# A max of three products rewritten around a product made once: x(W1Wo) + max(0, x(W2-W1), x(W3-W1))Wo

## The chip, the core and the metric

One core of one Trainium2 chip runs the whole program. Its engines have queues of their own: TensorE (PE, with PEld for its weight loads), VectorE (DVE), ScalarE (ACT), GpSimd (POOL) and SyncE (SP), which here only issues DMAs. The metric is the device time of one execution in microseconds, the median of several runs. All numbers are float32.

## The reference

A delta-rule attention block feeds a feed-forward block with a max over three products. Batch 4, 8 heads, 768 positions, head size 48; then 3072 tokens of 384 features, hidden size 768.

```python
for t in range(S):
    y[:, :, t] = einsum('bhd,bhde->bhe', q[:, :, t], state)
    v_old = einsum('bhde,bhd->bhe', state, kt)          # kt: normalized key
    state = state + bt * einsum('bhd,bhe->bhde', kt, vt - v_old)
x = y.transpose(0, 2, 1, 3).reshape(3072, 384)
h = maximum(maximum(x @ w1, x @ w2), x @ w3)
out = h @ w_out
```

## The kernel before

**Groups.** The sequence is cut into chunks of 64 positions. A "unit" of the recurrence is one chunk of all batches and heads, two units make a group, and a group is 512 tokens. There are six groups, 0 to 5. `ffn(m)` computes the feed-forward part of group m; it is a generator which yields after every step, and between its steps the attention of the next group is issued. So matmuls of the two parts alternate in TensorE's one queue in an order written out by hand.

**The feed-forward part.** `hidden(f, lo, w)` makes one of six tiles h (128 hidden features by 512 tokens): for each of w1, w2, w3 three matmuls into a PSUM tile p_h (L884), then a ScalarE copy for the first (L892) and a VectorE max for the other two (L894). After the six tiles, four output tiles p_o of 128 tokens are made by six matmuls each (L908), copied by ScalarE to o_sb (L916) and written to memory (L919). p_h and p_o share a PSUM ring of two tiles. A group from 1 on has 18 hidden steps and 4 output steps, numbered i = 0 to 21. Group 0 runs 18 half-wide hidden steps, 9 whole ones and 4 output steps, i = 0 to 30; weights are still being unpacked there.

**The attention around it.** The table `LINKS` says which pieces of attention are issued after step i of a group. A letter is a function, the digit a unit (or one of four key blocks). Those that matter here:

- k, q: `old_k`, `old_q`, the products of keys and queries with the state (p_k, p_q, L737); k also subtracts on VectorE (v_t, L749). s: `step`, the state update (p_s, st). u, z, j: `new`, `join_z`, `join_u`, the products that make u. y: `to_y` makes y (p_y, L805, and VectorE, L807). x: `y_blocks` sends y to memory as y_x (L837).
- w: `read_y` loads y back in another layout as y_q (L846). X: `turn_y` transposes y_q into half of xt, the next group's input, on VectorE (L857). Beside group 0 x is `to_x` instead, with TensorE transposes (p_x, L819), and w and X are not used.
- K, V: loads of later keys and values (L115, L131). p: `prep_sums` squares a unit's keys on ScalarE (ksq, L282), sums them on VectorE (L283) and exchanges the sums by DMA (ksum, L288). P: `prep_values` makes norms of them (L260 to L265) and scales v_t on GpSimd (L292).
- L, N: `load_blocks` loads blocks of keys on SyncE and of queries on GpSimd into tiles called turned (L401), from a ring of five tiles that y_q uses too. t: `turn_blocks` transposes them on VectorE (kqt, L417). g: `gram` multiplies them (p_g, L443) and sends the result to memory (at_d, L473).

**The triangular solve.** `solve(m)` reads at_d as x_bl and does, on VectorE alone, a set-up (L534 to L550) and 31 steps of two operations each (L564, L568), then sends y_d (L590) and loads ut from it (L599). `some(solving, n)` issues n of its steps. The loop over groups starts it after step 10 of groups 1 to 3 and spreads its steps over the rest of the group; its last two pieces, the ut loads, fall at the end. Group 4 issues no solve and no key loads, and group 5 has no attention beside it.

Of the kernel before, what the change touches and what calls it, by code (L numbers as in the profile page):

```python
# [12 lines left out]
ALU = mybir.AluOpType  # L13
# [8 lines left out]
def kernel(  # L22
# [31 lines left out]
    nc = tc.nc  # L54
# [3 lines left out]
    DM = H * D  # L58
    DFF = moe_w1.shape[1]
    KT = DM // 128  # L60
    FT = DFF // 128
# [16 lines left out]
    def ps_ffn(shape, name):  # L78
        return psum.tile(shape, FP32, name=name, tag="ffn", bufs=2)

    def ps_two(name):
        return psum.tile([128, 2, 512], FP32, name=name, tag="two", bufs=3)
# [4 lines left out]
    ident = const.tile([128, 128], FP32, name="ident")  # L87
# [16 lines left out]
    def rows(bb):  # L104
        return slice(C * bb, C * (bb + 1))
# [67 lines left out]
    for bb in range(2):  # L173
        nc.gpsimd.affine_select(
            out=mask[rows(bb)], in_=mask[rows(bb)], pattern=[[1, C]], base=-1,
# [10 lines left out]
    w_sb = [const.tile([128, KT, DFF], FP32, name=f"w{i}_sb") for i in range(3)]  # L186
    wo_sb = const.tile([128, FT, DM], FP32, name="wo_sb")
# [15 lines left out]
    def fetch(queue=nc.scalar):  # L203
        if fetched[0] < len(pieces):
            _, src, (a, b) = pieces[fetched[0]]
            st = work.tile([128, 2 * 384], U32, name="w_bits", bufs=5)
            queue.dma_start(
                out=st.rearrange("p (a b) -> p a b", a=a), in_=src
            )
            staged.append(st)  # L210
            fetched[0] += 1
# [63 lines left out]
    def prep_sums(c):  # L275


        ksum, kflip = small("ksum", 2, H), small("kflip", H)
        for g in range(2):
            kk = kpad[(2 * c + g) % NK][:, :, 0:D]  # L280
            ksq = work.tile([128, H, D], FP32, name="ksq", tag="o_sb")
            nc.scalar.square(ksq, kk)  # L282
            nc.vector.tensor_reduce(  # L283
                out=kflip if g else ksum[:, 0], in_=ksq,
                axis=mybir.AxisListType.X, op=ALU.add,
            )
        for bb in range(2):
            nc.sync.dma_start(out=ksum[rows(bb), 1], in_=kflip[rows(1 - bb)])  # L288
        sums[c] = ksum
# [59 lines left out]
    def square(name):  # L349
        return work.tile([128, H, C], FP32, name=name, tag="square", bufs=17)  # L350
# [39 lines left out]
    def load_blocks(n):  # L390
        c, g = divmod(n, 2)
        for i in range(2):
            t = turned[n, i] = work.tile(
                [128, 2, TURNED], FP32, name="turned", tag="w_bits", bufs=5
            )
            nc.gpsimd.memset(t[:, :, TURNED - 48 : TURNED], 0.0)  # L396
            for bb in range(2):
                for par in range(2):
                    for db in range(2):
                        p0, at = DP * par + 32 * db, 32 * (1 - db)  # L400
                        (nc.sync, nc.gpsimd)[i].dma_start(  # L401
                            out=t[p0 : p0 + 32, bb, at : at + NP * 2 * D].rearrange(
                                "p (j x) -> p j x", j=NP
                            ),
                            in_=(k, q)[i][
                                2 * bb + g, :, c * C : (c + 1) * C, :
                            ].rearrange(
                                "(j two) (r tb) d -> two r j (tb d)", two=2, tb=2
                            )[par],
                        )  # L410
# [459 lines left out]
            nc.vector.tensor_copy(to[:, 1], of[:, 1])  # L870


    def ffn(m):
        xt = xts[m]
        hs = {}

        def hidden(f, lo, w):
            if f not in hs:
                hs[f] = square("h").rearrange("p h c -> p (h c)")
            h = hs[f][:, lo : lo + w]  # L880
            for i in range(3):
                p_h = ps_ffn([128, TOK], "p_h")[:, 0:w]
                for t in range(KT):
                    nc.tensor.matmul(  # L884
                        p_h,
                        w_sb[i][:, t, f * 128 : (f + 1) * 128],
                        xt[:, t, lo : lo + w],
                        start=(t == 0),
                        stop=(t == KT - 1),
                    )  # L890
                if i == 0:
                    nc.scalar.copy(h, p_h)  # L892
                else:
                    nc.vector.tensor_tensor(out=h, in0=h, in1=p_h, op=ALU.max)  # L894
                yield


        early = FT // 2 if m == 0 else 0
        for lo in (0, TOK // 2):
            for f in range(early):  # L900
                yield from hidden(f, lo, TOK // 2)
        for f in range(early, FT):
            yield from hidden(f, 0, TOK)
        for i in range(4):
            cc, g = divmod(i, 2)
            p_o = ps_ffn([128, DM], "p_o")
            for f in range(FT):
                nc.tensor.matmul(  # L908
                    p_o,
                    hs[f][:, i * 128 : (i + 1) * 128],  # L910
                    wo_sb[:, f],
                    start=(f == 0),
                    stop=(f == FT - 1),
                )
            o_sb = work.tile([128, DM], FP32, name="o_sb")
            nc.scalar.copy(o_sb, p_o)  # L916
            for bb in range(2):
                tok0 = (2 * bb + g) * S + (2 * m + cc) * C
                nc.sync.dma_start(out=out[tok0 : tok0 + C, :], in_=o_sb[rows(bb)])  # L919
            yield  # L920
# [3 lines left out]
    def some(gen, n):  # L924
        for _ in range(n):
            if next(gen, gen) is gen:
                break
# [72 lines left out]
    for c in range(2):  # L1000
# [29 lines left out]

    LINKS = {
        0: "k0 q0 t0 L2", 1: "g0 t1 L3", 2: "g1 d0", 3: "z0 d1", 4: "z1 t2",
        5: "j0 g2", 6: "j1 t3", 7: "u0 g3", 9: "s0", 10: "y0", 11: "k1 q1 x0",
        12: "w0 V0", 13: "u1", 14: "K0 K1 V1", 15: "y1 x1 X0", 16: "K2 K3 p0",
        17: "s1 w1 p1", 18: "N0 P0", 19: "X1 P1", 20: "N1",
    }
    EARLY_LINKS = {
        9: "k0 q0", 10: "e0", 11: "e1 t0", 12: "f0 t1", 13: "f1 d0 g0",
# [20 lines left out]
    def links(m, names):  # L1059
        for name in names.split():  # L1060
            f, i = name[0], int(name[1])
            if f in RECURS and m < GROUPS:
                RECURS[f](2 * m + i)
            elif f in MADE and m + 1 < GROUPS:
                MADE[f](2 * (m + 1) + i)
            elif f in UNIT and m + 1 < GROUPS:
                UNIT[f](4 * (m + 1) + i)
            elif f == "N" and m + 2 < GROUPS:
                load_blocks(4 * (m + 2) + i)

    def queries(names):
        for name in names.split():
            f, n = name[0], int(name[1])
            if f not in OF_KEYS:
                links(0, name)
                continue
            OF_KEYS[f](n)
            if f == "T" and n + 3 < 11:
                load_q(n + 3)
# [4 lines left out]
    for i, _ in enumerate(ffn(0)):  # L1084
        if i - 1 in CONVERTED:
            fetch(nc.sync)
        queries(FIRST.get(i, ""))
        links(1, EARLY_LINKS.get(i, ""))
        if i in CONVERTED:
            some(conv, 1)  # L1090
        if i in (1, 2):
            prep_sums(i + 1)
        if i in (4, 5, 6):
            some(solving, (4, 2, 1)[i - 4])
        if i in (5, 7):
            prep_values(i // 2)
        if 7 <= i < 11:
            load_k(i + 1)
        if i == 0:
            load_v(3)  # L1100
        if i == 12:
            load_q(11)
        if i in (10, 18):
            load_v(4 + i // 18)
        if i in (11, 15):
            prep_sums(4 + i // 15)
        if i in (14, 20):
            prep_values(4 + i // 20)
        if i == 18:
            blocks(2)  # L1110
        if i == 21:
            solving = solve(2)
            some(solving, 1)
        if 21 < i < 27:
            some(solving, 3)
        if i >= 27:
            some(solving, 4 if i < 30 else 5)
        if i in (27, 28):
            load_blocks(i - 15)


    RECURS.update(x=y_blocks, w=read_y, X=turn_y)
    UNIT.update(t=turn_blocks)
    for m in range(1, GROUPS):
        for i, _ in enumerate(ffn(m)):
            if i < 2:
                some(solving, 1)
            if m + 2 < GROUPS:
                if i == 8:
                    blocks(m + 2)  # L1130
                if i == 10:
                    solving = solve(m + 2)
            steps = 4 if i >= 18 else 3
            if i > 10:
                some(solving, steps - 2)
            links(m + 1, LINKS.get(i, ""))
            if 10 <= i < 20:
                some(solving, 2)
    by_hand.close()
# [28 lines left out]
```

## Time and profile before

| | us |
|---|---|
| median of three runs | 574.99 |
| lowest, highest | 573.28, 579.36 |
| span of the profiled execution | 571.2 |
| PE busy | 536.1 |
| DVE busy | 358.1 |
| ACT busy | 145.4 |
| POOL busy | 127.1 |

The span runs from the first to the last instruction of the profiled execution; what lies around it is not in it. Where the groups stand, from the timeline of TensorE (start of the group's first p_h, in us from the span's start):

| group | 1 | 2 | 3 | 4 | 5 | end of the last p_o |
|---|---|---|---|---|---|---|
| start | 178.99 | 261.02 | 344.48 | 428.75 | 504.90 | 566.9 |

In the page, "busy" is the sum of an engine's instructions; a timeline line has start, duration, engine, line of the kernel, operation, output and inputs, shapes, count, and in square brackets how long the engine stood idle before it and what released it. SPq is SyncE's queue, where a duration is the time to issue.

### The profile page before, as it was taken

How to read it: one execution, taken by the hardware profiler on the slowest of the kernel's cores; microseconds unless marked ns; L12 is line 12 of the kernel's file. 1: busy time of each engine (PE TensorE's matmuls, PEld its weight loads, DVE VectorE, ACT ScalarE, POOL GpSimd, SP SyncE). 2: the span in 40 equal slices, each digit the busy share in tenths (PEclk: the TensorE clock that was granted, in tenths of full speed). 3: DMA queues.
4: the chain of work that ended last, by engine and by line, in shares of the span. 5: the costliest groups of instructions: out<-in, count | busy, mean ns of one | idle time of the engine just before them, and what ended most of it. 6: DMA issues, size and time to landing. Idle time of an engine off the chain costs nothing.

```text
span 571.2 us, 18729 instructions
## 1 busy us (share of the span) xinstructions
PE 536.1 (94%) x8102; PEld 317.1 (56%) x8102; DVE 358.1 (63%) x785; ACT 145.4 (25%) x282; POOL 127.1 (22%) x224
## 2 busy tenths in 40 slices
PE   6678779889999999999999999999999999999997
PEld 5567657765555555555555464555555555544453
DVE  6888998786997645996637995637994432201110
ACT  4455544455302221212121111221112201010001
POOL 7225235144540530016430017300011000000000
PEclk9656899989999999999999999999999999999999
DMA  8874467756035632645642846632834001310002
GB/s 111 173 162 122 94 161 137 176 120 159 9 74 129 134 71 74 115 113 143 136 84 67 136 99 161 125 57 64 136 88 90 3 12 48 78 33 1 0 0 55
DMA packets 149057, 53.54 MB, mean 94 GB/s; under 512 B 133296, under 2 KB 145392, under 8 KB 148976
## 3 DMA queue, kind: packets, MB, share of 16 engines
q1 hardware_dynamic: 143536, 47.13, 39.1%
q0 software_dynamic: 3328, 4.83, 3.7%
q8 instruction: 63, 1.03, 0.8%
q10 hardware_dynamic: 2112, 0.39, 0.5%
q14 instruction: 18, 0.15, 0.1%
HBM read 39.17 MB, written 13.11 MB: 92 GB/s over the span
## 4 chain that ended last, share of the span: by engine, by line
PE 65%; DVE 13%; DMA 9%; SPq 4%; issue 3%; ACT 2%; POOL 2%; ACTq 0%; DVEq 0%; POOLq 0%
PE p_h L884 40%; PE p_o L908 11%; DMA kpad<-in_k_dram 3%; DMA turned<-in_q_dram 3%; PE p_g L443 3%; DVE tmp L564 2%; SPq L115 2%; DVE y_bl L568 2%; PE p_u L765 2%; PE p_k L737 2%; PE p_y L805 1%; PE p_q L737 1%; PE p_s L787 1%; DMA v_t<-in_v_dram 1%; PE p_z L707 1%
## 5 line engine op out<-in xcount | busy, mean ns | idle before, releaser
L884 PE MATMUL p_h<-xt,w_sb 128*128 128x512 f32 (+1 forms) x702 | 303.4, 578 | 3.4 <-POOL w_sb L253 1.6
L884 PEld LDWEIGHTS p_h<-xt,w_sb 128*128 128x128 f32 x702 | 129.9, 194 | 124.5 <-issue 112.8
L894 DVE TENSOR_TENSOR h<-h,p_h 128x512 f32<-128x512 f32 (+1 forms) x78 | 50.1, 643 | 92.1 <-PE p_h L884 91.4
L908 PE MATMUL p_o<-wo_sb,h 128*128 128x384 f32 x288 | 94.4, 487 | 0.0
L908 PEld LDWEIGHTS p_o<-wo_sb,h 128*128 128x128 f32 x288 | 54.3, 190 | 37.5 <-issue 1.0
L292 POOL TENSOR_TENSOR v_t<-v_t,nrm 128x768 f32<-128x768 f32 x12 | 17.7, 1474 | 178.2 <-DMA out_dram<-o_sb 102.0
L568 DVE TENSOR_TENSOR y_bl<-y_bl,tmp 128x31 f32<-128x31 f32 (+20 forms) x139 | 53.7, 386 | 4.8
L401 POOL DMA_DIRECT2D turned<-in_q_dram x96 | 52.1, 550 | 5.0 <-POOL turned L396 3.8
L892 ACT COPY h<-p_h 128x512 f32<-128x512 f32 (+1 forms) x39 | 21.5, 550 | 110.9 <-PE p_h L884 109.0
L564 DVE TENSOR_TENSOR tmp<-x_bl,y_bl 128x31 f32<-128x31 f32 (+20 forms) x139 | 46.6, 335 | 3.8
L443 PE MATMUL p_g<-kqt 48*64 48x64 f32 (+1 forms) x1216 | 30.9, 241 | 15.5 <-issue 4.2
L443 PEld LDWEIGHTS p_g<-kqt 48*64 48x64 f32 x1216 | 25.7, 141 | 23.8 <-issue 9.0
L916 ACT COPY o_sb<-p_o 128x384 f32<-128x384 f32 x24 | 11.5, 478 | 88.1 <-PE p_o L908 80.8
L460 ACT COPY at<-p_g 128x512 f32<-128x512 f32 x21 | 12.3, 584 | 44.2 <-DVE pt L427 41.9
L230 POOL TENSOR_SCALAR mant<-mant 128x384 f32<-128x384 f32 x24 | 13.4, 557 | 39.1 <-ACT mant L226 38.4
L253 POOL TENSOR_TENSOR w_sb<-mant,up 128x384 int32<-128x384 int32 x18 | 17.9, 997 | 14.7 <-DVE mant L249 11.7
L427 DVE TENSOR_TENSOR pt<-p_g,mask 128x512 f32<-128x512 f32 x22 | 15.2, 690 | 8.7 <-PE p_g L443 8.5
L417 DVE STREAM_TRANSPOSE kqt<-turned 128x256 f32<-128x256 f32 x48 | 17.4, 416 | 4.7 <-DMA turned<-in_k_dram 4.4
L793 DVE TENSOR_TENSOR st<-st,p_s 128x768 f32<-128x768 f32 x11 | 10.5, 951 | 12.4 <-PE p_s L787 12.3
L680 DVE TENSOR_SCALAR ut<-p_j 32x512 f32<-32x512 f32 (+1 forms) x13 | 8.4, 648 | 15.6 <-ACT ut L682 15.5
L765 PEld LDWEIGHTS p_u<-v_t,ut 64*64 64x64 f32 x768 | 13.4, 142 | 8.2 <-issue 4.7
L805 PEld LDWEIGHTS p_y<-u,pt 64*64 64x64 f32 x768 | 13.1, 142 | 8.2 <-issue 6.8
(130 smaller groups left out, 520.4 us busy)
## 6 DMA issues: line engine op xcount, KB each, us to landing
w_bits<-in_moe_w_dram SPq DMA_DIRECT2D x18, 384.0 KB
v_t<-in_v_dram SPq DMA_DIRECT2D x24, 192.0 KB
turned<-in_q_dram POOLq DMA_DIRECT2D x96, 48.0 KB, 2.9
out_dram<-o_sb SPq DMA_DIRECT2D x48, 96.0 KB
turned<-in_k_dram SPq DMA_DIRECT2D x96, 48.0 KB
kpad<-in_k_dram SPq DMA_DIRECT2D x44, 96.0 KB
y_x<-y SPq DMA_DIRECT2D x16, 192.0 KB
y_q<-y_x SPq DMA_DIRECT2D x32, 96.0 KB
```

The source lines that it names most:

```text
L253: nc.gpsimd.tensor_tensor(out=dst.bitcast(I32), in0=mant_v.bitcast(I32), in1=up_v, op=ALU.add)
L292: nc.gpsimd.tensor_tensor(out=vts[c], in0=vts[c], in1=nrm[:, :, :, None].to_broadcast([128, 2, H, D]), op=ALU.mult,)
L401: (nc.sync, nc.gpsimd)[i].dma_start(out=t[p0 : p0 + 32, bb, at : at + NP * 2 * D].rearrange("p (j x) -> p j x", j=NP), in_=(k, q)[i][2 * b ...
L443: nc.tensor.matmul(p_g[rows(bb ^ (g * i)), par, c0 : c0 + C * (1 + whole)], kq[:, 0], kq if whole else kq[:, i],)
L564: nc.vector.tensor_tensor(out=t_v, in0=row.to_broadcast(t_v.shape), in1=column.to_broadcast(t_v.shape), op=ALU.mult,)
L568: nc.vector.tensor_tensor(out=rest, in0=rest, in1=t_v, op=ALU.subtract)
L765: nc.tensor.matmul(p_v[rows(bb ^ g), g, i], ut[c % NU][rows(bb), g, h], rhs[rows(bb), g, h],)
L805: nc.tensor.matmul(p_v[rows(bb), g, i], pt[g][r, h], u[r, g, h])
L884: nc.tensor.matmul(p_h, w_sb[i][:, t, f * 128 : (f + 1) * 128], xt[:, t, lo : lo + w], start=(t == 0), stop=(t == KT - 1),)
L892: nc.scalar.copy(h, p_h)
L894: nc.vector.tensor_tensor(out=h, in0=h, in1=p_h, op=ALU.max)
L908: nc.tensor.matmul(p_o, hs[f][:, i * 128 : (i + 1) * 128], wo_sb[:, f], start=(f == 0), stop=(f == FT - 1),)
```

## The change

The max is rewritten: max(a, b, c) = a + max(0, b-a, c-a), so that out = x(W1Wo) + max(0, x(W2-W1), x(W3-W1))Wo. From group 1 on a hidden tile needs two products, the first taken through a ReLU on ScalarE and the second by a VectorE max; each output tile gets three more matmuls, which add x(W1Wo). Group 0 is computed as before.

- `less_first` subtracts w1 from w2 and w3 in place, 128 columns at a time, after steps 18, 19, 20, 22, 25 and 27 of group 0 (two VectorE operations each).
- `turn_first` transposes w1 in place, after steps 27, 28 and 29 of group 0 (six TensorE transposes and two ScalarE copies each).
- `both_layers(t)` makes a third of W1Wo after steps 2, 5 and 8 of group 1 (six matmuls and a ScalarE copy each) and keeps it where w1 was.
- An output tile of a later group yields twice, after its fifth matmul and at its end. A group has 12 + 8 = 20 steps instead of 22; `LINKS` and the solve's pacing are written anew for that. In the table w1 now stands before K2 and K3, under one step, where it stood one step after them.

```diff
--- before.py
+++ after.py
@@ -870,6 +870,41 @@
             nc.vector.tensor_copy(to[:, 1], of[:, 1])
 
 
+    def less_first(f):
+        part = (slice(None), slice(None), slice(f * 128, (f + 1) * 128))
+        for i in (1, 2):
+            nc.vector.tensor_tensor(
+                out=w_sb[i][part], in0=w_sb[i][part], in1=w_sb[0][part],
+                op=ALU.subtract,
+            )
+
+    def turn_first(fs):
+        p_f = ps_two("p_t")
+        for i, f in enumerate(fs):
+            for t in range(KT):
+                nc.tensor.transpose(
+                    p_f[:, i, t * 128 : (t + 1) * 128],
+                    w_sb[0][:, t, f * 128 : (f + 1) * 128],
+                    ident,
+                )
+        for i, f in enumerate(fs):
+            nc.scalar.copy(
+                w_sb[0][:, :, f * 128 : (f + 1) * 128],
+                p_f[:, i, 0 : KT * 128].rearrange("p (t x) -> p t x", t=KT),
+            )
+
+    def both_layers(t):
+        p_m = ps_ffn([128, DM], "p_m")
+        for f in range(FT):
+            nc.tensor.matmul(
+                p_m,
+                w_sb[0][:, t, f * 128 : (f + 1) * 128],
+                wo_sb[:, f],
+                start=(f == 0),
+                stop=(f == FT - 1),
+            )
+        nc.scalar.copy(w_sb[0][:, t, 0:DM], p_m)
+
     def ffn(m):
         xt = xts[m]
         hs = {}
@@ -878,7 +913,7 @@
             if f not in hs:
                 hs[f] = square("h").rearrange("p h c -> p (h c)")
             h = hs[f][:, lo : lo + w]
-            for i in range(3):
+            for i in range(m > 0, 3):
                 p_h = ps_ffn([128, TOK], "p_h")[:, 0:w]
                 for t in range(KT):
                     nc.tensor.matmul(
@@ -890,6 +925,10 @@
                     )
                 if i == 0:
                     nc.scalar.copy(h, p_h)
+                elif m and i == 1:
+                    nc.scalar.activation(
+                        out=h, in_=p_h, func=mybir.ActivationFunctionType.Relu
+                    )
                 else:
                     nc.vector.tensor_tensor(out=h, in0=h, in1=p_h, op=ALU.max)
                 yield
@@ -904,14 +943,16 @@
         for i in range(4):
             cc, g = divmod(i, 2)
             p_o = ps_ffn([128, DM], "p_o")
-            for f in range(FT):
+            last = slice(i * 128, (i + 1) * 128)
+            terms = [(hs[f][:, last], wo_sb[:, f]) for f in range(FT)]
+            if m:
+                terms += [(xt[:, t, last], w_sb[0][:, t, 0:DM]) for t in range(KT)]
+            for n, (stays, moves) in enumerate(terms):
                 nc.tensor.matmul(
-                    p_o,
-                    hs[f][:, i * 128 : (i + 1) * 128],
-                    wo_sb[:, f],
-                    start=(f == 0),
-                    stop=(f == FT - 1),
+                    p_o, stays, moves, start=(n == 0), stop=(n == len(terms) - 1)
                 )
+                if m and n == 4:
+                    yield
             o_sb = work.tile([128, DM], FP32, name="o_sb")
             nc.scalar.copy(o_sb, p_o)
             for bb in range(2):
@@ -1030,9 +1071,9 @@
 
     LINKS = {
         0: "k0 q0 t0 L2", 1: "g0 t1 L3", 2: "g1 d0", 3: "z0 d1", 4: "z1 t2",
-        5: "j0 g2", 6: "j1 t3", 7: "u0 g3", 9: "s0", 10: "y0", 11: "k1 q1 x0",
-        12: "w0 V0", 13: "u1", 14: "K0 K1 V1", 15: "y1 x1 X0", 16: "K2 K3 p0",
-        17: "s1 w1 p1", 18: "N0 P0", 19: "X1 P1", 20: "N1",
+        5: "j0 g2", 6: "j1 t3", 7: "u0 g3", 8: "s0", 9: "y0", 10: "k1 q1 x0",
+        11: "w0 V0", 12: "u1", 13: "K0 K1 V1", 14: "y1 x1 X0", 15: "s1 w1 K2 K3 p0",
+        16: "p1", 17: "N0 P0", 18: "X1 P1", 19: "N1",
     }
     EARLY_LINKS = {
         9: "k0 q0", 10: "e0", 11: "e1 t0", 12: "f0 t1", 13: "f1 d0 g0",
@@ -1117,6 +1158,10 @@
             some(solving, 4 if i < 30 else 5)
         if i in (27, 28):
             load_blocks(i - 15)
+        if i in (18, 19, 20, 22, 25, 27):
+            less_first((18, 19, 20, 22, 25, 27).index(i))
+        if 27 <= i < 30:
+            turn_first((2 * (i - 27), 2 * (i - 27) + 1))
 
 
     RECURS.update(x=y_blocks, w=read_y, X=turn_y)
@@ -1125,16 +1170,18 @@
         for i, _ in enumerate(ffn(m)):
             if i < 2:
                 some(solving, 1)
+            if m == 1 and i in (2, 5, 8):
+                both_layers(i // 3)
             if m + 2 < GROUPS:
                 if i == 8:
                     blocks(m + 2)
                 if i == 10:
                     solving = solve(m + 2)
-            steps = 4 if i >= 18 else 3
+            steps = 4 if i > 11 else 3
             if i > 10:
                 some(solving, steps - 2)
             links(m + 1, LINKS.get(i, ""))
-            if 10 <= i < 20:
+            if 10 <= i < 19:
                 some(solving, 2)
     by_hand.close()
 # ---- launch: one core; inputs and outputs as the reference has them ----
```

## The prediction, on record before the run

> **What bounds the kernel now.** I read the busy slices first, then the chain of waits, then the timelines of one middle group. From the page: TensorE is full from about 145 us on, VectorE comes in bursts, and the chain that ended last is mostly TensorE.
>
> ```profile
> PE   6678779889999999999999999999999999999997
> DVE  6888998786997645996637995637994432201110
> PE 65%; DVE 13%; DMA 9%; SPq 4%; issue 3%; ACT 2%; POOL 2%; ACTq 0%; DVEq 0%; POOLq 0%
> ```
>
> So matmuls removed late are worth their time, as long as what lies under them still fits. I checked that in group 2. Its first p_h stands at 261.02 us; the next group's is the last line here (TensorE's timeline: start, duration):
>
> ```profile
> 307.61 1.15 PE L737 MATMUL p_k<-st,kqt 48*64 48x48 f32 x64
> ...
> 328.90 15.75 PE L908 MATMUL p_o<-wo_sb,h 128*128 128x384 f32 x48
> 344.48 2.74 PE L884 MATMUL p_h<-xt,w_sb 128*128 128x512 f32 x6
> 357.71 1.48 PE L443 MATMUL p_g<-kqt 48*64 48x64 f32 x62 [1.31 <-DVE kqt L417]
> ```
>
> I call the start of a group's first p_h S and the end of its second unit's p_k T (here 308.6; 0.97 after its start, when p_q begins). From T to the next S there are 35.9 us of unbroken matmuls. The next S also needs the second half of xt, which VectorE writes last, by L857. VectorE in that stretch:
>
> ```profile
> 333.71 0.55 DVE L283 TENSOR_REDUCE kflip<-ksq 128x8 f32<-128x384 f32 x1 [0.17 <-ACT ksq L282]
> ...
> 338.73 1.53 DVE L568 TENSOR_TENSOR y_bl<-y_bl,tmp 128x175 f32<-128x175 f32 x1
> ...
> 342.17 1.23 DVE L857 STREAM_TRANSPOSE xt<-y_q 128x768 f32<-128x768 f32 x1
> ```
>
> xt is ready at 343.4, 1.1 us before TensorE wants it, after a stretch in which VectorE had no pause over 0.2 us. TensorE bounds this stage, with hardly a margin. SyncE's queue and ScalarE beside it:
>
> ```profile
> 305.96 1.17 SPq L837 DMA_DIRECT2D y_x<-y  x2
> 312.77 2.55 SPq L846 DMA_DIRECT2D y_q<-y_x  x4
> ...
> 325.17 4.47 SPq L115 DMA_DIRECT2D kpad<-in_k_dram  x4
> ...
> 347.11 1.09 SPq L590 DMA_DIRECT2D y_d<-y_bl  x2
> 348.57 5.13 SPq L401 DMA_DIRECT2D turned<-in_k_dram  x8
> ...
> 355.29 4.42 SPq L599 DMA_DIRECT2D ut<-y_d  x8
> ```
> ```profile
> 333.16 0.52 ACT L282 ACTIVATE ksq<-kpad 128x384 f32<-128x384 f32 x1 [0.20 <-DMA kpad<-in_k_dram]
> ```
>
> y_q can be issued 6.8 us after y_x. The last keys are squared (end of ksq) 4.0 us after the end of their four issues (329.64 to 333.68), just as VectorE wants them.
>
> **What the Trainium skill says.** (1) Perfetto Trace Analysis, "Tensor Engine Instruction", says that ScalarE, VectorE and GpSimd queues are strict first-in first-out and that matmul ends are modelled. The trace agrees: kflip above waited and nothing overtook it; so I take matmul prices from the spacing of starts. (2) DMA: Bandwidth & Descriptors, "Anatomy of one DMA — SWDGE (gpsimd) path", says that semaphore waits happen on the issuing sequencer before dispatch, so a queue stands still. SyncE waited for y_x eight times, 26.9 us in all. (3) SBUF — State Buffer, "SBUF: two separate sides", says that a GpSimd operation and a VectorE one with two SBUF inputs exclude each other. The trace agrees: the L568 above took 1.53 where its neighbour of 156 took 0.32, while v_t scaling (L292, 1.47) ran on GpSimd.
>
> **The change part by part.** Prices from spacing: three p_h matmuls 2.57 (group 5: 46.35/18), one p_o matmul 0.64 (15.48/24), 0.2 more where small matmuls follow.
>
> *Removed.* Per group from 1 on, six p_h: 6 x 2.57 = 15.4. *Added*: 12 p_o-like matmuls, 12 x 0.64 = 7.7. Net -7.7 on TensorE in each of five groups, -38.5. ReLU on ScalarE costs like its copy (0.585), under a 2.57 step, and VectorE loses six max operations a group.
>
> *Once.* W1Wo: 18 matmuls x 0.64 = 11.5 on TensorE, in group 1; three copies of 0.48 on ScalarE hide under the following p_h. 18 transposes at 0.14 (p_x: six in 0.84) = 2.5, plus 0.5 of switching, in group 0; their six ScalarE copies lie beside p_o. Twelve subtractions on VectorE: the trace has none of 384 elements from SBUF; the 252-element one takes 0.42 and the 31-element one 0.19, so about 0.56 each, 6.7 in all. Bounds: 0 (hidden) to 6.7 on the path. VectorE is nearly full from 146 on and p_h there already waited for it (0.48 at 152.47), so the fourth pair (1.1) and part of the fifth show: I take 2. Group 0: +5 (3 to 10).
>
> *The tail, T to next S, groups 1 to 3.* TensorE now needs q 1.0, one p_h 2.6, 36 p_o 23.0, three small batches 3.2 and switches 0.7: T+30.5. VectorE: from memset (222.64 in group 1) to the second L857 (258.55) it worked 35.9 without pause; off come four max operations (0.6 each) and v_t (0.87), which now goes ahead of it; on come two solving steps now ahead of L857 (1.0): 33.7. The memset can start at T+1.2, so xt would be ready at T+1.2+33.7+1.1 = T+36.0 even if VectorE never waited: 5.5 late.
>
> It will wait. The instruction order of the changed kernel has, on SyncE: first output (now inside the tail), keys 0 and 1, v, y_x, second output, y_q, and only then keys 2 and 3; the table put w1 ahead of K2 K3. Step by step: the first p_o ends at T+10.7, its copy at T+11.5, output issued to 12.7, keys (3.2) to 15.9, v to 17.3. VectorE has y ready at T+16.8, so y_x is issued at 17.3, y_q at 17.3+6.8 = 24.1 to 26.7, keys 2 and 3 (3.8 to 4.5; 4.2) to 30.9, second ksq done at 34.9. VectorE reaches the second pair of sums at about T+26 and stands till 34.9; behind it are four solving steps, the norm, four more steps (7.8 in all by the timeline, one at GpSimd's price of 1.2 more) and L857: T+43.8. ScalarE stands too, with the third o_sb copy behind ksq; its buffer is wanted at the next S only. So next S = T+44, 13.5 later than TensorE could, of which VectorE's work is 5.5 and SyncE's order 7.9.
>
> *The head, S to T.* Clean, the old head takes 46.4 (47.56 in group 2 less its stall of 1.1); less one p_h: 43.8. In groups 2 and 3 there is a second new wait. N1's keys ("turned", 8 issues) used to be issued before the ut loads; in the new order they come after: solving ends about S+2.4 as before, y_d is issued then, ut after y_d landed (431.04 to 434.10: 3.1) at S+5.5, eight issues 5.0 to S+10.5, turned 4.5 to S+15.0, landing 2.6 (269.92 to the L417 at 272.58), two L417 more: p_g at S+18.4 instead of S+12.4 and S+13.2. TensorE reaches it at S+11.3, so it stalls 7.1. T = S+50.9. In group 1 those blocks were loaded in group 0; T = 46.1 - 2.6 + 11.5 = S+55.0.
>
> Groups, old to new: 1: 82.0 to 99.0 (+17.0). 2: 83.5 to 94.9 (+11.4). 3: 84.3 to 94.9 (+10.6). 4, which solves nothing and loads no keys: 76.1 to 68.4 (-7.7); its last xt is ready at about T+29.0 (y_x 16.3, +6.8, +4.7 from y_q to L857 as at 492.04, 1.2) against TensorE's 29.2, so no stall. 5: -7.7. Group 0: +5. **Sum +28.6.** The profiled execution spans 571.2; the runs' median is 575.0, 3.8 more, which I keep: 571.2 + 28.6 + 3.8 = **603.6, about 604**.
>
> POOL's queue keeps its order; its v_t scaling and loads follow the later norms and are in the 1.2 and the head above.
>
> **The rivals.**
>
> *The bound stays with TensorE (faster).* If xt were ready by T+30.5 in every group and p_g never late: +5 + 11.5 - 38.5 = -22, 553. For it: TensorE is full and the sum of VectorE is only 63%. Against: 35.9 us of VectorE work must shrink below 30, and the order takes off 3. It decides from the point where VectorE works less than about 28 us between memset and L857.
>
> *VectorE alone is late.* If neither DMA wait shows: 553 + 3 x 5.5 = 570, no change to be measured. Needs keys 2 and 3 squared by T+26; SyncE would have to issue them before y_x lands.
>
> *One of the two DMA waits fails to show.* Without the late turned keys: 604 - 14 = 590. Without the wait for keys 2 and 3: 604 - 3 x 7.9 = 580.
>
> *The change does less than it says.* The order shows 12 hidden steps in each later group and the added matmuls, so this is out.
>
> *More goes wrong.* Subtractions wholly on the path, DMAs slower when bunched: 610 to 620.
>
> **How the numbers follow.** A measurement here tells about 1% from no change (569 to 581). Chances: both waits as priced, 596 to 611: 0.57; only one of them: 0.19 (of it 0.03 near 580 within 1%); VectorE alone: 0.08; TensorE: 0.09; worse: 0.07. Time 604; range 580 to 612, leaving out TensorE, VectorE alone and some of the worst. Faster 0.10, same 0.10, slower 0.80.
>
> **What would show it.** Right: VectorE idle some 8 us before its second pair of L283 sums, released by ScalarE's ksq and that by kpad; TensorE idle 13 us ahead of the first p_h of groups 2 to 4, released by L857; SyncE's kpad issue right behind y_q; p_g of groups 2 and 3 waiting for L417, that for turned; groups 4 and 5 shorter by 7.7. Wrong: first p_h with no gap, TensorE full as before (then 553), or gaps with VectorE busy throughout (570).

## The result, and the profile after

The changed kernel took 602.64 us (median of four runs, 600.28 to 605.52) against 576.02 for the kernel before (its three runs of the table and a fourth, 573.28 to 579.36): a ratio of 1.0447, 95% interval 1.0384 to 1.0510. It is slower, as forecast, at 604 us in the prediction. The profiled execution spans 603.5, 32.3 more than before; the medians lie 26.6 apart, and the predicted sum of 28.6 lies between the two.

The page of the changed kernel first: busy tenths of TensorE and VectorE in 40 slices of 15.1 us, the granted TensorE clock in tenths, and the shares of the chain that ended last.

```profile
PE   6479877989999999992699993879996599999997
DVE  6877997769996432977353796445496642111100
PEclk9755998979999999996989998879999699999999
...
PE 59%; DVE 18%; DMA 9%; SPq 7%; issue 3%; ACT 3%; POOL 1%; DVEq 0%; ACTq 0%; POOLq 0%
```

TensorE's unbroken row of nines now has three dips (to 2, 3 and 5), one ahead of each of the groups 2, 3 and 4, and each time VectorE is at 7 or more shortly before. In the chain TensorE fell from 65% to 59% and VectorE rose from 13% to 18%. The third row is the one that I had not thought of: the clock dips with the work.

How long each group takes, from the start of its first p_h to the next one's (TensorE's timelines; for group 0 from the span's start, for group 5 to the end of the last p_o). The last three rows are experiments and are explained there:

| us | group 0 | 1 | 2 | 3 | 4 | 5 |
|---|---|---|---|---|---|---|
| before | 179.0 | 82.0 | 83.5 | 84.3 | 76.1 | 62.0 |
| predicted | 184.0 | 99.0 | 94.9 | 94.9 | 68.4 | 54.3 |
| after | 185.4 | 97.4 | 95.6 | 96.0 | 70.5 | 54.4 |
| e3, both orders put back | 183.9 | 93.2 | 83.9 | 84.5 | 70.8 | 54.4 |
| e6, e3 with sums and solve earlier | 186.7 | 86.3 | 76.1 | 78.0 | 68.5 | 54.3 |
| e8, kernel before with e6's order | 181.9 | 82.2 | 82.2 | 82.2 | 76.2 | 62.0 |

**The pause ahead of a group.** TensorE's timeline around the end of the tail of group 2 (T, the end of that group's second p_k, is at 336.52, where p_q begins; the profile has two records for each p_h or p_o matmul, so x6 is three of them):

```profile
335.55 1.15 PE L737 MATMUL p_k<-st,kqt 48*64 48x48 f32 x64
336.52 1.11 PE L737 MATMUL p_q<-st,kqt 48*64 48x48 f32 x64
...
365.35 2.10 PE L951 MATMUL p_o<-w_sb,xt 128*128 128x384 f32 x6
378.45 4.78 PE L919 MATMUL p_h<-xt,w_sb 128*128 128x512 f32 x6 [11.00 <-DVE newton L261]
```

The last p_o ends at about 367.3, T+30.8, and then TensorE stands for 11.0 us. The releaser is printed as newton (L261), but that instruction only follows L857 in VectorE's queue: what p_h takes is xt. VectorE's timeline says why xt is late:

```profile
360.33 0.55 DVE L283 TENSOR_REDUCE kflip<-ksq 128x8 f32<-128x384 f32 x1 [0.59 <-ACT ksq L282]
...
367.86 0.55 DVE L283 TENSOR_REDUCE ksum<-ksq 128x8 f32<-128x384 f32 x1 [3.61 <-ACT ksq L282]
369.26 0.55 DVE L283 TENSOR_REDUCE kflip<-ksq 128x8 f32<-128x384 f32 x1 [0.85 <-ACT ksq L282]
...
377.12 1.18 DVE L857 STREAM_TRANSPOSE xt<-y_q 128x768 f32<-128x768 f32 x1
378.23 0.13 DVE L261 TENSOR_SCALAR newton<-root 128x16 f32<-128x16 f32 x1
```

It waited 0.59 + 3.61 + 0.85 = 5.05 us for squared keys, and every step of the solve behind these sums, and L857 too, stands behind that. The 0.59, at the first pair of sums, is of another kind: it stays in e1 and e3, where SyncE's order is put back. ScalarE's timeline names what the squaring had waited for, and SyncE's shows where those keys stood in its queue (start, time to issue):

```profile
367.30 0.52 ACT L282 ACTIVATE ksq<-kpad 128x384 f32<-128x384 f32 x1 [7.01 <-DMA kpad<-in_k_dram]
```
```profile
353.80 1.16 SPq L837 DMA_DIRECT2D y_x<-y  x2
355.11 2.47 SPq L960 DMA_DIRECT2D out_dram<-o_sb  x2
360.77 2.56 SPq L846 DMA_DIRECT2D y_q<-y_x  x4
363.38 2.70 SPq L115 DMA_DIRECT2D kpad<-in_k_dram  x4
```

The key loads need nothing of y. They stand behind y_q, which waits until y_x has landed, so SyncE issues nothing from 357.6 to 360.8.

**The stall in the head.** SyncE's and TensorE's timelines from the start of group 2 (S = 282.81):

```profile
285.35 1.25 SPq L590 DMA_DIRECT2D y_d<-y_bl  x2
...
288.29 6.54 SPq L599 DMA_DIRECT2D ut<-y_d  x8
295.20 7.44 SPq L401 DMA_DIRECT2D turned<-in_k_dram  x16
```
```profile
299.13 0.30 PE L443 MATMUL p_g<-kqt 48*64 48x64 f32 x2 [2.91 <-DVE kqt L417]
301.23 2.31 PE L443 MATMUL p_g<-kqt 48*64 48x64 f32 x62 [1.81 <-DVE kqt L417]
303.47 4.74 PE L919 MATMUL p_h<-xt,w_sb 128*128 128x512 f32 x6
```

The key blocks follow the eight ut loads, and the second part of p_g starts at S+18.4, the prediction's own figure. Behind each of these two pauses the six p_h records took 4.7 to 4.8 us, where they took 2.74 to 2.84 before.

### The profile page after: what moved, and what is told of

The parts are those of the page before. It is cut to its first block, busy times and chain, and to the rows that moved or that the text cites. A ratio compares the mean times of both kernels' runs of the same rounds, so it can differ in the third digit from the quotient of the medians.

```text
span 603.5 us, 18673 instructions
## 1 busy us (share of the span) xinstructions
PE 523.5 (87%) x8096; PEld 320.2 (53%) x8096; DVE 344.8 (57%) x767; ACT 149.2 (25%) x291; POOL 128.3 (21%) x224
## 4 chain that ended last, share of the span: by engine, by line
PE 59%; DVE 18%; DMA 9%; SPq 7%; issue 3%; ACT 3%; POOL 1%; DVEq 0%; ACTq 0%; POOLq 0%
PE p_h L919 30%; PE p_o L951 12%; DMA kpad<-in_k_dram 4%; DMA y_x<-y 3%; DVE tmp L564 3%; PE p_g L443 3%; DVE y_bl L568 3%; SPq L115 2%; PE p_m L899 2%; PE p_k L737 1%; PE p_u L765 1%; PE p_y L805 1%; SPq L401 1%; PE p_j L720 1%; SPq L846 1%
## 5 line engine op out<-in xcount | busy, mean ns | idle before, releaser
L919 PE MATMUL p_h<-xt,w_sb 128*128 128x512 f32 (+1 forms) x522 | 232.8, 589 | 38.6 <-DVE newton L261 33.8
L919 PEld LDWEIGHTS p_h<-xt,w_sb 128*128 128x128 f32 x522 | 99.7, 202 | 127.3 <-issue 117.5
L951 PE MATMUL p_o<-wo_sb,h 128*128 128x384 f32 x288 | 99.4, 490 | 0.0
L933 DVE TENSOR_TENSOR h<-h,p_h 128x512 f32<-128x512 f32 (+1 forms) x48 | 29.7, 618 | 58.1 <-PE p_h L919 57.8
L929 ACT ACTIVATE h<-p_h 128x512 f32<-128x512 f32 x30 | 17.9, 597 | 116.2 <-PE p_h L919 116.2
L443 PEld LDWEIGHTS p_g<-kqt 48*64 48x64 f32 x1216 | 27.1, 146 | 28.7 <-issue 12.0
L951 PE MATMUL p_o<-w_sb,xt 128*128 128x384 f32 x120 | 42.0, 486 | 0.0
L957 ACT COPY o_sb<-p_o 128x384 f32<-128x384 f32 x24 | 11.4, 476 | 89.5 <-PE p_o L951 83.3
L951 PEld LDWEIGHTS p_o<-w_sb,xt 128*128 128x128 f32 x120 | 22.8, 190 | 15.9
L427 DVE TENSOR_TENSOR pt<-p_g,mask 128x512 f32<-128x512 f32 x22 | 15.2, 690 | 18.6 <-PE p_g L443 18.4
L749 DVE TENSOR_TENSOR v_t<-v_t,p_k 128x768 f32<-128x768 f32 x11 | 10.5, 952 | 25.0 <-PE p_k L737 25.0
L417 DVE STREAM_TRANSPOSE kqt<-turned 128x256 f32<-128x256 f32 x48 | 17.3, 416 | 11.7 <-DMA turned<-in_k_dram 11.5
L230 POOL TENSOR_SCALAR mant<-mant 128x384 f32<-128x384 f32 x24 | 13.4, 557 | 44.0 <-ACT mant L226 44.0
L253 POOL TENSOR_TENSOR w_sb<-mant,up 128x384 int32<-128x384 int32 x18 | 18.0, 997 | 14.5 <-DVE mant L249 11.5
```

What stands on the lines that cost most here:

```text
L253: nc.gpsimd.tensor_tensor(out=dst.bitcast(I32), in0=mant_v.bitcast(I32), in1=up_v, op=ALU.add)
L417: nc.vector.transpose(out=kqts[n][:, :, bb ^ (n % 2), i].rearrange("p j (r tb) -> p j tb r", tb=2), in_=t[:, bb, 32 : 32 + NP * 2 * D].rea ...
L427: engine.tensor_tensor(out=by_par(t), in0=of, in1=mask[:, None, None, :].to_broadcast([128, 2, NP, C]), op=ALU.mult,)
L443: nc.tensor.matmul(p_g[rows(bb ^ (g * i)), par, c0 : c0 + C * (1 + whole)], kq[:, 0], kq if whole else kq[:, i],)
L919: nc.tensor.matmul(p_h, w_sb[i][:, t, f * 128 : (f + 1) * 128], xt[:, t, lo : lo + w], start=(t == 0), stop=(t == KT - 1),)
L929: nc.scalar.activation(out=h, in_=p_h, func=mybir.ActivationFunctionType.Relu)
```

## The experiments

Two theories stood at the start. **A**: the loss is two places in SyncE's order (keys behind y_q, key blocks behind ut), and besides them VectorE's own work ahead of xt. **B**: it is VectorE's load alone, or something that the rewriting itself costs, and the order doesn't matter.

### e1, the keys ahead of y

```diff
-        15: "s1 w1 K2 K3 p0",
+        15: "s1 K2 K3 w1 p0",
```

> Keys 2 and 3 are issued ahead of the read of y_q, the rest as changed. Theory A (SyncE's order makes VectorE wait for the sums): the waits of VectorE before the second pair of L283 sums, 5.05 us in group 2's tail, fall below 1, so three tails are 4 to 5 us shorter: 589, at least 586. Theory B (VectorE's own work alone is late, the wait only lies beside it): 602, no change. Theory C (the keys are late from a busy DMA, not from the order): the sums still wait, 600 to 603.

586.25 us, ratio to the kernel before 1.0147 (1.0079 to 1.0215): 16.4 off the changed kernel's 602.64. VectorE's waits at the second pair of sums fell to 0.3 us or less. The pauses ahead of groups 2 to 4 fell from 11 to 6.82, 6.68 and 6.75; the stall at p_g stayed (2.48 + 1.79 in group 2). A's share for this order holds.

### e2, the key blocks ahead of ut

At step 19 the last two pieces of the solve, the ut loads, are issued behind the step's links instead of ahead of them.

```diff
-            if i > 10:
+            if 10 < i < 19:
                 some(solving, steps - 2)
             links(m + 1, LINKS.get(i, ""))
-            if 10 <= i < 19:
+            if 10 <= i:
                 some(solving, 2)
```

> The key blocks N1 are issued between y_d and the ut loads, as in the kernel before; the rest as changed. Theory A (queue order): p_g of groups 2 and 3 starts about 12.5 us after the group's start instead of 18.4, and the slow matmuls behind the pause go too: 6 + 2.7 us in two groups, 585. If ut then is late for p_z, some of it comes back: 590. Theory C (the blocks wait for a busy DMA or for their ring of tiles, not for the ut loads ahead of them): 602.

590.17, ratio 1.0214 (1.0157 to 1.0272): 12.5 off. p_g no longer waits in group 2 and only 0.33 in group 3; the pauses stay at 11.4, 11.3 and 12.0. It is what the prediction gives for the case without late key blocks, 590, but not the 585 expected of this run, and not for the reason named with 590 there: p_z waits for nothing. The stall that went was 4.7 us and not 6, and groups 2 and 3 are shorter by 7.3 and 6.3 where 8.7 each was expected.

### e3, both

> Both edits together. Theory A: the gains add, 602.6 - 13 - 18 = 571, and what is left of the pause before a group's first p_h is VectorE's own work, about 6 us in groups 2 to 4. If the two waits hid each other, less than the sum: 580. Theory B and C: 600.

576.35, ratio 0.9989 (0.9969 to 1.0009): level with the kernel before. The two gains nearly add (28.9 singly, 26.3 together); the 571 expected had e2's gain at 18, and e2 gave 12.5. What is left ahead of xt is, it seems, VectorE's own work, which e5 tests: in the tail of group 1 it waits just 0.59 + 0.41 us, and TensorE still stands 7.07, 6.42 and 7.09 us. TensorE's timeline at the start of group 2:

```profile
277.09 5.41 PE L919 MATMUL p_h<-xt,w_sb 128*128 128x512 f32 x6 [7.07 <-DVE newton L261]
```

So the order was the loss against the kernel before, and it was not all that kept the saved matmuls from showing.

### e4, the order alone, in the kernel before

Is the order costly without any of the new arithmetic? The kernel before, with its key loads moved behind y_q, and the sums of their squares, p0, with them:

```diff
-        15: "y1 x1 X0", 16: "K2 K3 p0",
-        17: "s1 w1 p1",
+        15: "y1 x1 X0", 16: "",
+        17: "s1 w1 K2 K3 p0 p1",
```

> The kernel before the change, with one edit: keys 2 and 3 are loaded after the read of y_q (one step later). No arithmetic of the change is in it. Theory A: VectorE stands about 7 us in each of three tails, of which 1.1 is margin, and matmuls run slowly for 2 us after each pause: 575 + 3 x 8 = 599. Rival (the loss comes from the matmuls that were taken away and added, not from the order): 575.

591.81, ratio 1.0232 (1.0168 to 1.0297), some 15 us slower than before: the order costs that without any of the new arithmetic. It fell short of A's 599, and in a way that A had not said: VectorE waits 5.0 to 6.1 us in each tail, not 7. TensorE's timeline at the end of group 1:

```profile
258.23 8.01 PE L908 MATMUL p_o<-wo_sb,h 128*128 128x384 f32 x24 [2.15 <-ACT o_sb L916]
267.64 2.81 PE L884 MATMUL p_h<-xt,w_sb 128*128 128x512 f32 x6 [1.40 <-DVE newton L261]
```

The late keys hold ScalarE at ksq, o_sb stands behind it, and so p_o waits for its PSUM tile: 2.15 us at p_o and 1.40 at p_h, where one wait at p_h was expected. In group 2 all of it, 3.25 us, falls at p_o.

### e5, the sums ahead of the tail

On top of e3, the K loads go to GpSimd's queue after steps 5 and 6, and the sums of squares (p0, p1) follow steps 8 and 9, so that neither is in the tail.

```diff
-        5: "j0 g2", 6: "j1 t3", ... 8: "s0", 9: "y0",
-        ... 13: "K0 K1 V1", ... 15: "s1 w1 K2 K3 p0", 16: "p1",
+        5: "j0 g2 K0 K1", 6: "j1 t3 K2 K3", ... 8: "s0 p0", 9: "y0 p1",
+        ... 13: "V1", ... 15: "s1 w1",
-    UNIT = dict(t=turn, g=gram, K=load_k, L=load_blocks)
+    UNIT = dict(t=turn, g=gram, K=lambda n: load_k(n, (nc.gpsimd,) * 2), L=load_blocks)
```

> On top of both orders: the four key loads are issued from GpSimd's queue after steps 5 and 6, and their squares and sums (L282, L283) stand after steps 8 and 9, ahead of the tail. VectorE loses four reductions (4 x 0.46) and a wait of 0.6 in each of three tails. Theory A (what is left of the pause is VectorE's own work, one for one): pause 6.7 to 4.3, 576.4 - 7 = 569. Theory B (what is left is the path of y through memory to y_q): pause unchanged, 576.

568.36, ratio 0.9848 (0.9802 to 0.9895), and the pauses are 3.94, 3.95 and 3.96. Sums (4 x 0.46) and waits for them, together 2.4 to 2.9 us, went out of VectorE's tail, and the pause is shorter by 2.5 to 3.1: nearly one for one, as it must be if VectorE's work is the next bound. The path of y through memory is not it. In return p_g waits about 1 us for key blocks in groups 2 and 3.

### e6, the solve one step earlier too

On top of e5, the solve starts after step 9 instead of 10, the norms (P0, P1) go behind X1, and the blocks N0 and N1 are loaded after step 16. What each of the three is worth was not measured singly.

```diff
-        17: "N0 P0", 18: "X1 P1", 19: "N1",
+        16: "N0 N1", 18: "X1 P0 P1",
-                if i == 10:
+                if i == 9:
                     solving = solve(m + 2)
-            if 10 <= i:
-                some(solving, 2)
+            if 9 <= i:
+                some(solving, 2 - (i == 18))
```

> On top of that: the solve starts one step earlier, the norms P0 and P1 stand behind the last transpose of xt, and the blocks N0 and N1 are loaded two and three steps earlier. VectorE gains about 3 us of lead and loses 1.0 to 2.2 us of norm ahead of xt. Theory A: the pause before groups 2 to 4 falls under 1 us and the slow matmuls behind it go, 576.4 - 3 x 8.9 = 550, near the sum for TensorE alone (553). If x_bl is not there in time the solve waits and 560 is left. Theory B: 569 as before it.

557.13, ratio 0.9654 (0.9599 to 0.9709): faster than both kernels. TensorE's timeline at group 2, and the busy tenths from the page:

```profile
273.02 2.81 PE L919 MATMUL p_h<-xt,w_sb 128*128 128x512 f32 x6 [0.24 <-DVE newton L261]
...
296.69 1.33 PE L443 MATMUL p_g<-kqt 48*64 48x128 f32 x32 [0.76 <-DVE kqt L417]
```
```profile
PE   6657787889999999999999999999999999999996
```

The nines are unbroken again from 125 us on. It missed the 550 expected by 7 us. Of these the profile names 4.9: p_g waits 0.76 in group 2 and 1.30 in group 3 for key blocks, the three p_h 0.9 together, and behind the 1.30 a p_g batch of 1.82 instead of 1.10 and a p_h of 4.00 instead of 2.84 ran at a lower clock (below).

### e7, the pause filled with matmuls

Does the slow clock behind a pause cost anything in the end? e3, with 28 matmuls of the identity, which nothing reads, after step 19 of groups 1 to 3.

```diff
+            if i == 19 and 0 < m < 4:
+                busy(28, ident)
```

> Both orders, and 28 matmuls of 128 columns that nothing reads, placed on TensorE behind the last p_o of groups 1 to 3, about 6 us of work in a pause of 6.4 to 7.1. Theory D (after a pause TensorE runs at a lower granted clock, which makes the first p_h take 4.4 to 5.4 instead of 2.7): p_h back at 2.7 and 3 x 2.2 = 6.6 less, 570. Rival (the first p_h is slow for want of xt or of a PSUM tile, not of clock): 576 or more.

TensorE's timeline:

```profile
271.58 6.41 PE L982 MATMUL p_w<-ident 128*128 128x128 f32 x56
278.20 2.81 PE L919 MATMUL p_h<-xt,w_sb 128*128 128x512 f32 x6 [0.20 <-DVE newton L261]
...
290.39 0.29 PE L443 MATMUL p_g<-kqt 48*64 48x64 f32 x2 [0.79 <-DVE kqt L417]
...
291.92 1.48 PE L443 MATMUL p_g<-kqt 48*64 48x64 f32 x62 [1.24 <-DVE kqt L417]
```

p_h is back at 2.81 us: the clock stays up if TensorE works through the pause. The time is 576.60, ratio 0.9994 (0.9968 to 1.0019), the same as e3's. So the theory of the clock was right, and the 570 that it gave was not. The next bound stood right behind: p_g in group 2 waits 0.79 + 1.24 = 2.03 us for key blocks, where e3 waited nothing there. Only group 4, which loads no keys, keeps the gain (68.8 us against 70.8). In the two profiled executions groups 1 to 4 together differ by 1.5 us, below what the medians resolve. So the slow first matmuls explain lines of the profile and hardly any of the time while xt and the key blocks come late anyway.

### e8, the new order without the new arithmetic

e6 is faster than the kernel before, but is that the rewriting or only a better order? e6's table, queue and solve in the kernel before, its arithmetic untouched:

```diff
-        5: "j0 g2", 6: "j1 t3", ... 9: "s0", 10: "y0",
-        ... 14: "K0 K1 V1", ... 16: "K2 K3 p0",
-        17: "s1 w1 p1", 18: "N0 P0", 19: "X1 P1", 20: "N1",
+        5: "j0 g2 K0 K1", 6: "j1 t3 K2 K3", ... 9: "s0 p0", 10: "y0 p1",
+        ... 14: "V1", ... 17: "s1 w1",
+        18: "N0 N1", 19: "X1 P0 P1",
```

> This is the kernel before, its arithmetic untouched, with the schedule of e6 alone: the K loads on GpSimd's queue and ahead of y, the two pairs of sums at steps 9 and 10, the solve's first four pieces at step 18 and its last ones with N1's key blocks at step 19. Theory A (the gain of e6 over the kernel before is the arithmetic's, and the order only lets it through): TensorE bounds the kernel before, and the only waits that the order can take away are those at p_h and p_g, some 3 us in all: 572 to 576 us. Rival B (the order by itself is what is faster, and the rewriting adds little): about 557 us, level with e6. Between the two, each share is read off: 576 less this run is the order's, this run less 557 the arithmetic's.

572.36, ratio 0.9899 (0.9828 to 0.9969). Its three middle groups take 82.2 us each, no first p_h and no p_g waits in them, and in the page its chain that ended last is mostly TensorE:

```profile
PE 81%; DVE 9%; ACT 3%; issue 2%; DMA 2%; SPq 2%; ACTq 0%; POOL 0%; DVEq 0%; POOLq 0%
```

Theory A: the order by itself is worth about 1% here (0.3 to 1.7), and the 3.4 us of group time that it saves are what groups 2 and 3 had lost. The arithmetic, on top of it, is worth 572.4 - 557.1 = 15.2 us, or 14 by the two ratios to the kernel before.

## Why the prediction was right

**The bound moved from TensorE to VectorE's xt.** Right. The tail's own matmuls end at T+30.8 (predicted T+30.5), taking 1.93 us for the last batch, the spacing of such batches. L857 ended at T+41.8; less the 5.05 us that VectorE waited it is T+36.7 (predicted T+36.0 if it never waits). e5 and e6, which take work out of that stretch, shorten the pause to 4 us and then to 0.44 at most.

**SyncE's order in the tail.** Right in place and chain, too large in size. At the second pair of sums VectorE waited 3.61 + 0.85 = 4.46 us, where the prediction has it stand from T+26 to T+34.9. y_x (T+17.3) and y_q (T+24.2) were issued when predicted, but keys 2 and 3 took 2.70 us to issue, where I took 4.2 from a range of 3.8 to 4.5. They were squared 3.1 us after that instead of 4.0, and VectorE reached the sums at 364.25, T+27.7. The price that I gave the order, 7.9 us in each group, is 16.4 / 3 = 5.5 by e1, with what it brings behind it.

**The key blocks behind ut.** Right, p_g at S+18.4, though to the tenth by luck: the ut loads took 6.5 us to issue instead of 5.0, and the key blocks behind them took 3.7 and 1.5 us to be issued and to land, priced at 4.5 and 2.6. The stall itself was 2.91 + 1.81 = 4.7 us, not 7.1, because TensorE arrived at S+13.4 instead of S+11.3: its first matmuls were slow, which I had not priced. e2 gives 12.5 us for two groups.

**What removed and added matmuls cost.** Right in the later groups, too large in group 0. With xt in time, e6 against e8 shows the two arithmetics under one order: group 4 is shorter by 7.6 us and group 5 by 7.7 (predicted 7.7), group 1 longer by 4.2 (predicted 11.5 - 7.7 = 3.8). Group 0's length says little, because its early part varies between executions: TensorE began the first whole p_h, ahead of any added instruction, at 127.38 us in the kernel before and at 130.97 in the changed one. From there to group 1 it took 51.6 us in all three profiled kernels with the old arithmetic and 54.4 in all seven with the new. So the change costs 2.8 us there, not 5. Each of the three batches of transposes takes 0.65 (2.0 in all, predicted 3.0), and p_h waits 0.8 more for VectorE (predicted 2).

**The term that was missing.** After each pause TensorE's clock was lower. The Trainium skill has it (TensorE: Matmul & The Clock Gate, "What's actually happening"): the default state is throttled, and about 3.4 us without work bring TensorE back to half rate until it has worked about as long. The trace agrees: 4.78 us behind 11.0 us of pause, against 2.74. A pause of 13 us was in my sum, and this should have been. Group 4 shows it undisguised: shorter by 5.7 instead of 7.7. In group 2 the slow first p_h only shortened the stall at p_g, and it was the slow matmuls behind that stall which lengthened the head: p_g took 2.31 instead of 1.48 and its p_h 4.74 instead of 2.84.

**Where luck came in.** In group 2 the tail was priced 2.1 us too long (44 against 41.9) and the head 2.8 too short (50.9 against 53.7). Over all groups, errors of +3.8 us remain (span of the groups, measured less predicted), of which 3.6 are the early part of group 0. The change's own errors run from -2.2 in group 0 and -1.6 in group 1 to +2.1 in group 4 and cancel to 0.2. So the mechanism was right, and that the total came so close is in part chance.

**The rivals.** "VectorE alone is late" (570) is e3, at 576.35: as that case says, no difference can be measured, and 2 us of slow matmuls at each of three pauses is about as much as its figure lacks. That these are the cause isn't shown: e7 took them away and the time stayed. "The bound stays with TensorE" (553) fell for the kernel as it was changed, and its price was nearly right for a kernel that meets its condition: e6, 557.13.

The 4 us above it are of the size of the waits and the lower clock named under e6, 4.9. Whether key blocks loaded earlier still would bring them wasn't tried.

## What to carry to other kernels

When matmuls are taken out of a stage where TensorE has no pause, first add up what the other engines do under it: here VectorE needed some 36 us under matmuls that shrank to 30, and a saving of some 20 us became a loss of 27. When steps are renumbered in a hand-written order, look at each queue for a load that needs nothing and now stands behind a DMA that waits for another; putting two such loads back was worth 26 us, more than the arithmetic. The saving is then had only after VectorE's work has been moved out of the short stretch, and the old arithmetic under the new order tells how much of the gain was order.

## What the runs showed of the hardware

The clock after a pause, in windows of the changed kernel and of e7 (window; length, then busy time and count for PE, PEld, DVE, ACT and POOL; granted clock, DMA share, GB/s):

```profile
337.00:367.30 30.30, 30.30 (x314) 18.07 (x306) 24.74 (x61) 3.91 (x8) 0.00 (x0) 1.00 0.53 114
367.30:378.40 11.10, 0.15 (x1) 0.00 (x0) 9.04 (x26) 2.22 (x6) 1.48 (x1) 0.72 0.28 61
378.40:384.00 5.60, 5.55 (x62) 2.69 (x66) 2.41 (x6) 0.60 (x1) 4.30 (x8) 0.64 0.29 58
```
```profile
276.00:280.00 4.00, 3.79 (x23) 2.68 (x23) 3.73 (x12) 0.00 (x0) 0.84 (x1) 1.00 0.26 66
```

From 1.00 it falls to 0.64 in the 5.6 us behind an 11 us pause, and stays at 1.00 where the pause was filled. The length of a pause didn't decide alone. In e4, pauses of 2.15 and 1.40 with 8 us of matmuls between left p_h at 2.81, and one of 3.25 in group 2 was followed by a clock of 0.59 over 4 us and by p_o records that took 9.70 instead of 8.01:

```profile
348.04 9.70 PE L908 MATMUL p_o<-wo_sb,h 128*128 128x384 f32 x24 [3.25 <-ACT o_sb L916]
```

In e6 a pause of 1.30 us, behind 64 records of small p_j matmuls, was followed by this window and by six p_h records of 4.00 us:

```profile
375.00:376.00 1.00, 1.00 (x4) 0.50 (x2) 0.69 (x1) 0.13 (x1) 0.00 (x0) 0.50 0.13 27
```

The idle window of about 3.4 us that the Trainium skill gives (TensorE: Matmul & The Clock Gate, "What's actually happening") doesn't cover that one: a pause far below it was enough. Whether small matmuls count less as work than large ones was not tried, and the cause stays open.
